# Attention and mixture of experts on one core: banks, probability, scaling and weight splits in another order

## The chip, the core and the metric

The kernel runs on one core of a Trainium2 chip. The metric is the device time of one execution in microseconds (us). Engines go by the profile's names: PE is TensorE (matmuls and transposes), DVE VectorE, ACT ScalarE, POOL GpSimd and SP SyncE; the last two mostly issue transfers here. Before the change the median of three runs is 726.74 us (725.18 to 727.03).

## What is computed

Attention in chunks of 64 tokens over 8 batches, 8 heads and 576 tokens gives 4608 tokens of 512 numbers. A layer of eight experts follows: each token goes through the expert that the gate, or the token before it, names, and the result is scaled with the gate's probability of that expert.

```python
x = attention(q, k, v)                    # (8, 576, 512), in chunks of 64
logits = x @ w_gate                       # 8 experts
e = argmax(logits[b, s]) if s == 0 or sigmoid(x[b, s] @ w_local) < 0.5 else prev_e
p = exp(logits - max); p /= sum(p) + 1e-9
h = maximum(x[b, s] @ w1[e], 0)           # 512 -> 1024
out[b, s] = p[e] * (h @ w2[e])            # 1024 -> 512
```

## The kernel before

The first part of the span (to about 215 us) is the attention, the gate and the sorting of tokens by expert. Then come **units**, numbered u = 0 to 23 here: `step(u)` is called for each in a loop over u, and later calls find nothing to do. A unit holds up to two tiles of 128 tokens of one expert. Its kind is read at run time from a table into registers, and branches select the work:

- a **pair** unit has two full tiles: u = 1, 3, 5 to 8, 10, 13, 14, 17 to 19, 22, 23. `couple` (L788) does the first layer of both tiles in 96 matmuls of 256 columns, in four groups of 24, one PSUM bank each. The results are split into a high and a low part, ACT's `activation` (L806) and DVE's `scalar_tensor_tensor` (L809).
- a **single** unit has one tile (u = 12, 15, 21; u = 0 does this without a branch): 24 matmuls (L656), then transposes in `single` (L768).
- a **partial** unit has up to 64 tokens (u = 11, 16, 20) or 32 (u = 2, 4, 9), the first of an expert. It multiplies the raw weights (L664, L677), while the weights are split for the units behind it.

Every product of a pair or single unit is made of three passes with split operands: weights `w1h`, `w1l` and `w2h`, `w2l` (high and low), tokens `xpp`, hidden values `hab` and `hb`. `split` (L106) makes a quarter of a weight: an ACT cast (L107) of the high part, then a DVE subtraction (L108) of the low one. `refill(0, u)` splits w1 and `refill(1, u)` w2 behind a branch on `turn[u]` (L1038): it is taken where the next unit starts another expert, after u = 1, 3, 8, 10, 14, 15 and 19. If the next unit is partial, `refill(0, u)` makes three quarters, and `partial` in `upper_layer` makes the fourth in the next unit. `reload` fetches raw weights of a later expert.

The order of the work on each engine is the order of the program text (a manual schedule); no planner moves it. For one unit it is: the gate's probability of u (`prob_atoms`, L640 to L647, with one exponential on ACT, L642); the first layer; `x_parts(u+1)`, which transposes the next unit's tokens on PE (L746, one bank of four transposes or two) and splits or copies them (L719, L720, L724, L725); the gather for u+2; `refill(0, u)`; `reload(0, u)`; `lower_layer(u-1)`, the second layer (L670 or L677) of the unit before, its scaling on DVE (L1121, or L703 to L706) and its scatter (L820 on POOL); `hidden(u)`, which for a pair runs `refill(1, u-1)` and then the second layer of the pair's first tile, called **y0** here, scaled at L1151, and for the rest transposes the hidden values and runs `refill(1, u-1)`.

A tile's readers wait by counts of finished instructions on the engine that wrote it. A tile that was written in a branch is ready for its readers when the writer's engine is past that branch, taken or not: these waits show in the trace as DVEq or ACTq L1038.

Of the kernel before, what the change touches and what calls it, by code (L numbers as in the profile page):

```python
# [14 lines left out]
ALU = mybir.AluOpType  # L15
# [3 lines left out]
ET = mybir.EngineType  # L19
# [13 lines left out]
NU = E + (N + (E - 1) * (P - 1)) // (2 * P)  # L33
UMIN = N // (2 * P) - 1
LAST = UMIN + 7
# [36 lines left out]
def tile_attention_then_moe(ctx: ExitStack, tc, q, k_in, v, wg, wl, w1, w2, out):  # L72
# [18 lines left out]
    w1h = [wpool.tile([P, F], F32R, name=f"w1h{c}") for c in range(4)]  # L91
# [14 lines left out]
    def split(hi, lo, raw, lo_eng=None):  # L106
        nc.scalar.copy(hi, raw)  # L107
        (lo_eng or nc.vector).tensor_tensor(lo, raw, hi.bitcast(F32), ALU.subtract)  # L108
# [229 lines left out]
    V = nc.vector  # L338
# [8 lines left out]
    def trp():  # L347
        return ps_tr.tile([P, 512], F32, name="tr")
# [150 lines left out]
    def run(fns):  # L499
        for fn in fns:  # L500
            fn()
# [129 lines left out]
    def prob_atoms(xg, hot):  # L631
        k = xg.shape[1]
        Lg = xg[:, :, C:C + E]
        m = pc.tile([P, 2], F32, name="pm")[:, 0:k]
        ex = pc.tile([P, 2, 2, E], F32, name="pex")[:, :, 0:k]
        sm = pc.tile([P, 2, 2], F32, name="psm")[:, :, 0:k]
        pr = pc.tile([P, 2], F32, name="ppr", bufs=4)
        wide = [P, k, E]
        return pr, [
            lambda: V.tensor_reduce(m, Lg, AX.X, ALU.max),  # L640
            lambda: V.tensor_tensor(ex[:, 0], Lg, m.unsqueeze(2).to_broadcast(wide), ALU.subtract),  # L641
            lambda: nc.scalar.activation(ex[:, 0], ex[:, 0], AF.Exp),  # L642
            lambda: V.tensor_tensor(ex[:, 1], ex[:, 0], hot.unsqueeze(1).to_broadcast(wide), ALU.mult),
            lambda: V.tensor_reduce(sm, ex, AX.X, ALU.add),  # L644
            lambda: V.tensor_scalar(m, sm[:, 0], 1e-9, None, ALU.add),
            lambda: V.reciprocal(m, m),
            lambda: V.tensor_tensor(pr[:, 2 - k:2], sm[:, 1], m, ALU.mult),  # L647
        ]
# [24 lines left out]
    def mm2_part(hf, y, fs):  # L673
        n = C // 2
        for f in fs:
            for j in range(2):
                nc.tensor.matmul(y[HT * j:HT * j + HT, 0:n], hf[:, f % 4, HT * (f // 4):HT * (f // 4) + HT],  # L677
                                 raw2[f // 2][:, f % 2, n * j:n * j + n], start=(f == 0), stop=(f == 7))
# [22 lines left out]
    def y_part(ysb, y, pr):  # L701
        n = C // 2
        V.memset(ysb[HT:P], 0.0)  # L703
        V.tensor_scalar(ysb[0:HT, 0:n], y[0:HT, 0:n], pr[0:HT], None, ALU.mult)
        V.tensor_copy(ysb[0:HT, n:C], y[HT:P, 0:n])
        V.tensor_scalar(ysb[0:HT, n:C], ysb[0:HT, n:C], pr[0:HT], None, ALU.mult)  # L706
# [82 lines left out]
        either(kind[u] and kind[u][1], plain, partial, True)  # L789

    def couple(u, hs):
        banks = [trp(), trp()] + hs
        dsts = h_slot(0), hps[u]
        for g, ps in enumerate(banks):
            for m in range(2):
                f = 2 * g + m
                for c in range(4):
                    for n, (a, w) in enumerate(PASSES):
                        nc.tensor.matmul(  # L799
                            ps[:, 256 * m:256 * m + 256], W1[w][c][:, P * f:P * f + P],  # L800
                            xpp[:, a, c].rearrange("p t q -> p (t q)"),
                            start=(c == 0 and n == 0), stop=(c == 3 and n == 2))
            ps = ps.rearrange("p (f t q) -> p t f q", f=2, t=2)
            parts = [[d[g // 2][a][:, g % 2 * 2:g % 2 * 2 + 2] for a in range(2)] for d in dsts]
            for half in range(2):
                nc.scalar.activation(parts[half][0], ps[:, half], AF.Relu)  # L806
            for half in range(2):
                hi, lo = parts[half]
                V.scalar_tensor_tensor(lo, ps[:, half], 0.0, hi.bitcast(F32), ALU.max, ALU.subtract)  # L809

    def new_ysb(own=False):
        return pc.tile([P, C], F32, name="ysb", **own_tag("ysb", own))
# [235 lines left out]
    def sub(v, engines):  # L1048
        hs = type(v.val)([h for h in v.val.handles if h.engine in engines])
        return type(v).of_register_unchecked(hs, min_val=0, max_val=3)  # L1050
# [17 lines left out]

    def kind_of(u):
        v = flag(3, u, [ET.PE, ET.Activation, ET.DVE, ET.Pool])  # L1070
        return v, sub(v, [ET.PE, ET.Activation, ET.DVE]), sub(v, [ET.Activation, ET.DVE])

    @contextmanager
    def when(v, otherwise=None):
# [11 lines left out]
    def upper_layer(u):  # L1086
        hs, hsb = new_h()
        v = kind[u] and kind[u][1]
        xg = xgs["u", u]
        prc[u], atoms = prob_atoms(xg if v is not None else xg[:, 1:2], ehot[:, u])  # L1090
        run(atoms)

        def plain():
            for c in range(4):
                mm1(x_slot(1), hs, c)
            relu(hsb, hs)

        def partial(M):
            mm1_part(xfs[u], hs, M)
            relu_part(hsb, hs, M)  # L1100
            split(w1h[3], w1l[3], raw1[3])

        if v is None:
            plain()
        else:
            with tc.If(v > 0) as cmp:
                either(v, plain, partial, True)
            with cmp.Else():
                couple(u, hs)
        return hsb  # L1110

    def lower_layer(u):
        y = new_y()
        keep = u + 1 == LAST
        ysb = new_ysb(u + 1 > LAST)
        pr = prc[u][:, 1:2]

        def plain():
            for c in range(4):
                mm2(hps[u], y, c)  # L1120
            V.tensor_scalar(ysb, y, pr, None, ALU.mult)  # L1121

        def partial():
            mm2_part(hfs[u], y, range(8))
            y_part(ysb, y, pr)

        with when(ok[u], (lambda: V.memset(ysb, 0.0)) if keep else None):
            either(kind[u] and kind[u][1], plain, partial)
            if not keep:
                put_y(q_of[u], ysb)  # L1130
        if keep:
            kept.append((q_of[u], ysb))

    def hidden(u, hsb):
        def second():
            if u:
                refill(1, u - 1)

        if kind[u] is None:
            single(u, hsb)  # L1140
            second()
            return
        with tc.If(kind[u][0] > 0) as cmp:
            single(u, hsb)
            second()
        with cmp.Else():
            second()
            y, ysb = new_y(0), new_ysb(u > LAST)
            for c in range(4):
                mm2(h_slot(0), y, c)  # L1150
            V.tensor_scalar(ysb, y, prc[u][:, 0:1], None, ALU.mult)  # L1151
            put_y(q_of[u] - 1, ysb)

    def step(u):
        if u == LAST + 1:
            with when(ok[u]):
                gather_full(u + 1)
        if u < NU:
            hps[u] = h_slot(1, u % 2)
            hfs[u] = pc.tile([P, 4, P], F32, name="hf", **own_tag("hf", u == LAST))  # L1160
            with when(ok[u]):
                hsb = upper_layer(u)
                if u + 1 < NU:
                    xfs[u + 1] = x_parts(u + 1)
        if u != LAST and u + 2 < NU:
            with when(ok[u + 1]):
                gather_full(u + 2)
        if u + 1 < NU:
            refill(0, u)
            reload(0, u)  # L1170
        if u + 2 < NU:
            if u + 2 not in kind:
                kind[u + 2] = kind_of(u + 2)
            turns(u + 1)
        lower_layer(u - 1)
        if u < NU:
            with when(ok[u]):
                hidden(u, hsb)
            if u:
                reload(1, u - 1)  # L1180

# [3 lines left out]
    with tc.manual_schedule(engines=MAN | {ET.SP, ET.Pool}):  # L1185
        kind, ok = {-1: None, 0: None, 1: kind_of(1)}, {u: None for u in range(-1, UMIN)}
        q_of = {u: Q0 + 2 * u + 1 for u in range(NU)} | {-1: EARLY - 1}
        hps[-1], hfs[-1], prc[-1] = h_slot(0), None, prc["e", EARLY - 1]
        turns(0)
        play(PAR["seam"], queues, part_played)  # L1190
        for u in range(LAST + 1):
            step(u)
            n = u + UMIN - 8
            if UMIN <= n < NU:
                ok[n] = valid(n)
                kind[n] = kind_of(n)
            run([sl[0:2], sl[2:3]][u] if u < 2 else [])
        with when(ok[LAST]):
            for u in range(LAST + 1, NU + 1):
                step(u)  # L1200
        for q, ysb in reversed(kept):
            put_y(q, ysb)
# [21 lines left out]
```

## Time and profile before

| | us |
|---|---|
| median of three runs | 726.74 |
| profiled execution, device time | 726.0 |
| its span | 724.1 |
| PE busy in the span | 639.8 (88%) |
| DVE busy | 352.8 (49%) |
| ACT busy | 244.3 (34%) |
| POOL busy | 157.1 (22%) |
| units, 215.0 to 724.1: length | 509.1 |
| units: PE busy | 449.5 |

The profiled execution spent 1.9 us outside its span, and its mean granted PE clock is 0.952 of full speed. PE works through every unit in turn, and the other engines serve it. What counts is therefore how long PE stands still between two pieces of its work, and in which stretches its granted clock is 0.50, where a matmul takes twice as long. The rows of that are in the section behind the next one.

### The profile page before, as it was taken

The numbers are of one execution on the slowest core, as the hardware profiler recorded it, in microseconds if no ns is written. First come the engines' busy times: TensorE is split into PE (matmuls) and PEld (weight loads), VectorE is DVE, ScalarE is ACT, GpSimd is POOL, SyncE is SP. The second block draws the span as 40 slices with busy tenths as digits, with TensorE's granted clock in tenths as the row PEclk, the third lists the DMA queues.
The fourth block names the chain that finished last, engine by engine and source line by source line (L and its number), as shares of the span: only waits on it lengthen the run. The fifth ranks groups of instructions, "written<-read, shape, count | busy, mean of one in ns | idle before, by whom it ended". The sixth has DMA issues, their size and how long they took to land. (4 is left out here: it accounts for less than half of the span.)

```text
span 724.1 us, 16913 instructions
## 1 busy us (share of the span) xinstructions
PE 639.8 (88%) x6136; PEld 530.1 (73%) x6136; DVE 352.8 (49%) x909; ACT 244.3 (34%) x461; POOL 157.1 (22%) x226
## 2 busy tenths in 40 slices
PE   6789999889899797799999797899987999979993
PEld 5668788666689585588889594698756798668882
DVE  3656778866966444253223354642464432353220
ACT  4557777563123132141113132420343221242110
POOL 4313232740231211112111211212021112121101
PEclk9989999999999988899999899999997999999997
DMA  8999999997141143614011242751336231055000
GB/s 225 244 228 241 243 248 271 265 315 236 59 161 47 42 151 92 218 49 164 31 47 45 61 158 69 249 170 60 134 95 238 76 125 60 31 174 174 31 19 34
DMA packets 103571, 100.98 MB, mean 139 GB/s; under 512 B 42488, under 2 KB 79352, under 8 KB 103416
## 3 DMA queue, kind: packets, MB, share of 16 engines
q1 hardware_dynamic: 88584, 61.01, 30.3%
q0 software_dynamic: 7440, 23.32, 9.9%
q10 hardware_dynamic: 7392, 14.68, 6.3%
q8 instruction: 85, 1.39, 0.8%
q14 instruction: 70, 0.57, 0.3%
HBM read 79.95 MB, written 20.35 MB: 139 GB/s over the span
## 5 line engine op out<-in xcount | busy, mean ns | idle before, releaser
L670 PE MATMUL y<-w2h,hab 128*128 128x512 f32 x432 | 149.1, 418 | 5.7 <-ACTq L1038 3.9
L820 POOL DMA_INDIRECT out<-ysb,sidx x41 | 41.0, 1001 | 363.3 <-DVEq L1038 160.2
L670 PEld LDWEIGHTS y<-w2h,hab 128*128 128x128 f32 x432 | 86.6, 201 | 29.1 <-ACTq L1038 5.6
L670 PE MATMUL y<-w2l,hab 128*128 128x512 f32 x216 | 91.4, 423 | 17.8 <-DVEq L1038 17.8
L799 PE MATMUL tr<-xpp,w1h 128*128 128x256 f32 x448 | 84.8, 287 | 3.1 <-DVE hf L173 1.9
L799 PE MATMUL h<-xpp,w1h 128*128 128x256 f32 x448 | 82.9, 283 | 0.0
L642 ACT ACTIVATE pex<-pex 128x16 f32<-128x16 f32 (+1 forms) x27 | 5.9, 217 | 205.1 <-DVE pex L641 184.4
L799 PEld LDWEIGHTS tr<-xpp,w1h 128*128 128x128 f32 x448 | 71.9, 194 | 3.8 <-ACT hf L171 2.1
L799 PEld LDWEIGHTS h<-xpp,w1h 128*128 128x128 f32 x448 | 70.8, 192 | 0.0
L670 PEld LDWEIGHTS y<-w2l,hab 128*128 128x128 f32 x216 | 43.3, 201 | 32.6 <-DVEq L1038 23.1
L799 PE MATMUL tr<-xpp,w1l 128*128 128x256 f32 x224 | 64.2, 286 | 0.0
L626 POOL DMA_INDIRECT xg<-x_d,gidx x49 | 48.4, 988 | 70.0 <-DVE psm L644 31.6
L799 PE MATMUL h<-xpp,w1l 128*128 128x256 f32 x224 | 63.4, 283 | 0.0
L1151 DVE TENSOR_SCALAR ysb<-y,ppr 128x512 f32<-128x512 f32 x14 | 10.5, 751 | 86.8 <-PE y L670 86.8
L1121 DVE TENSOR_SCALAR ysb<-y,ppr 128x512 f32<-128x512 f32 x19 | 14.3, 750 | 70.0 <-PE y L670 55.9
L746 PE MATMUL tr<-ident,xg 128*128 128x128 f32 x156 | 24.8, 295 | 21.6 <-issue 18.4
L799 PEld LDWEIGHTS tr<-xpp,w1l 128*128 128x128 f32 x224 | 43.5, 194 | 0.4
L670 PE MATMUL y<-w2h,hb 128*128 128x512 f32 x128 | 43.6, 412 | 0.0
L799 PEld LDWEIGHTS h<-xpp,w1l 128*128 128x128 f32 x224 | 42.9, 192 | 0.0
L809 DVE SCALAR_TENSOR_TENSOR hab<-h,hab 128x256 fp32r<-128x256 f32 x44 | 17.1, 420 | 50.7 <-ACT hab L806 27.9
L108 DVE TENSOR_TENSOR w1l<-raw,w1h 128x1024 fp32r<-128x1024 f32 x28 | 33.0, 1221 | 12.7 <-ACT w1h L107 12.6
L746 PEld LDWEIGHTS tr<-ident,xg 128*128 128x128 f32 x156 | 18.9, 150 | 27.6 <-issue 22.4
(259 smaller groups left out, 1142.3 us busy)
## 6 DMA issues: line engine op xcount, KB each, us to landing
raw<-in_moe_w SPq DMA_DIRECT2D x14, 1024.0 KB
raw<-in_moe_w ACTq DMA_DIRECT2D x14, 1024.0 KB
raw<-in_moe_w SPq DMA_DIRECT2D x16, 512.0 KB
qt<-in_q SPq DMA_DIRECT2D x11, 512.0 KB
kt<-in_k SPq DMA_DIRECT2D x11, 512.0 KB
v<-in_v SPq DMA_DIRECT2D x22, 256.0 KB
x_d<-xs SPq DMA_DIRECT2D x7, 521.0 KB
x_d<-x_w2h SPq DMA_DIRECT2D x6, 521.0 KB
```

The costliest lines, as they stand in the source:

```text
L108: (lo_eng or nc.vector).tensor_tensor(lo, raw, hi.bitcast(F32), ALU.subtract)
L626: nc.gpsimd.indirect_dma_start(out=dst, out_offset=None, in_=src, in_offset=bass.IndirectOffsetOnAxis(ap=gidx[t].bitcast(U32), axis=0))
L642: lambda: nc.scalar.activation(ex[:, 0], ex[:, 0], AF.Exp),
L670: nc.tensor.matmul(y, hx[f // 4][a][:, f % 4], W2[w][c][:, f % 2, :], start=(f == 0 and n == 0), stop=(f == 7 and n == 2))
L746: nc.tensor.transpose(ps[:, n], xg[:, half, P * n:P * n + P], ident)
L799: nc.tensor.matmul(ps[:, 256 * m:256 * m + 256], W1[w][c][:, P * f:P * f + P], xpp[:, a, c].rearrange("p t q -> p (t q)"), start=(c == 0 a ...
L809: V.scalar_tensor_tensor(lo, ps[:, half], 0.0, hi.bitcast(F32), ALU.max, ALU.subtract)
L820: nc.gpsimd.indirect_dma_start(out=out, out_offset=bass.IndirectOffsetOnAxis(ap=sidx[t].bitcast(U32), axis=0), in_=ysb, in_offset=None, bo ...
L1121: V.tensor_scalar(ysb, y, pr, None, ALU.mult)
L1151: V.tensor_scalar(ysb, y, prc[u][:, 0:1], None, ALU.mult)
```

## The change

Six things stand elsewhere in the program. (1) `couple` fills the two `h` banks first and the two `tr` banks last. (2) The probability of u moves from the start of the unit to `side_work(u)`, behind `x_parts(u+1)`. (3) So does the fourth quarter of the w1 split, in a branch of its own (L1136), and `refill(0, u)` of units that are not pairs. (4) For pairs `refill(0, u)` moves into the pair's branch of `hidden(u)`, behind `refill(1, u-1)`. (5) The scaling and the scatter of u-1 become `lower_out` and stand behind `hidden(u)`. (6) `reload(0, u)` comes at the end of the step. Two further registers hold the kind for PE alone and for DVE alone, as the branches of `lower_layer` and `lower_out` are now taken apart. No matmul, cast, subtraction, scaling or transfer is added or removed. Of branch instructions executed there are more: on DVE 257 compares for 219 and 254 jumps for 209, on ACT 258 and 254 for 243 and 209, on PE 171 and 245 for 164 and 209.

```diff
     def couple(u, hs):
-        banks = [trp(), trp()] + hs
+        banks = hs + [trp(), trp()]
...
     def upper_layer(u):
         hs, hsb = new_h()
         v = kind[u] and kind[u][1]
-        xg = xgs["u", u]
-        prc[u], atoms = prob_atoms(xg if v is not None else xg[:, 1:2], ehot[:, u])
-        run(atoms)
...
         def partial(M):
             mm1_part(xfs[u], hs, M)
             relu_part(hsb, hs, M)
-            split(w1h[3], w1l[3], raw1[3])
...
+    def side_work(u):
+        xg = xgs["u", u]
+        prc[u], atoms = prob_atoms(xg if kind[u] else xg[:, 1:2], ehot[:, u])
+        run(atoms)
+        if kind[u]:
+            with tc.If(kind[u][2] > 0):
+                with tc.If(kind[u][2] > 1):
+                    split(w1h[3], w1l[3], raw1[3])
+                renew(0, u)
+        else:
+            renew(0, u)
...
         with tc.If(kind[u][0] > 0) as cmp:
             single(u, hsb)
-            second()
+            renew(1, u - 1)
         with cmp.Else():
-            second()
+            renew(1, u - 1)
+            renew(0, u)
             y, ysb = new_y(0), new_ysb(u > LAST)
...
                     xfs[u + 1] = x_parts(u + 1)
+                side_work(u)
...
-        if u + 1 < NU:
-            refill(0, u)
-            reload(0, u)
...
-        lower_layer(u - 1)
+        run(more)
+        y = lower_layer(u - 1)
         if u < NU:
             with when(ok[u]):
                 hidden(u, hsb)
+        lower_out(u - 1, y)
+        if u < NU:
+            if u + 1 < NU:
+                reload(0, u)
             if u:
                 reload(1, u - 1)
```

In the rows below a name stands for an instruction's output and inputs: `ysb` a scaled tile, `y` its PSUM bank, `raw` raw weights, `tr` and `h` banks of PSUM.

First DVE at the end of `hidden(3)`, in the program before: the branch of `refill(1, 2)` in the pair's half, then y0's scaling.

```order
L1038 COMPARE_AND_BRANCH
L108 TENSOR_TENSOR w2l<-raw_0_85,w2h 128x1024 x2
L108 TENSOR_TENSOR w2l<-raw_1_86,w2h 128x1024 x2
L1038 UNCONDITIONAL_BRANCH x2
L1151 TENSOR_SCALAR ysb<-y,ppr 128x512
L1143 UNCONDITIONAL_BRANCH
L1059 UNCONDITIONAL_BRANCH
```

The same place in the program after, from behind `refill(1, 2)`; the scaling of unit 2 (L703 to L706 or L1124) follows these rows.

```order
L1038 COMPARE_AND_BRANCH
L108 TENSOR_TENSOR w1l_77<-raw_0_83,w1h_73 128x1024
L108 TENSOR_TENSOR w1l_78<-raw_0_83,w1h_74 128x1024
L108 TENSOR_TENSOR w1l_79<-raw_1_84,w1h_75 128x1024
L1078 COMPARE_AND_BRANCH
L108 TENSOR_TENSOR w1l_80<-raw_1_84,w1h_76 128x1024
L1078 UNCONDITIONAL_BRANCH x2
L1038 UNCONDITIONAL_BRANCH
L1159 TENSOR_SCALAR ysb<-y,ppr 128x512
L1150 UNCONDITIONAL_BRANCH
L1059 UNCONDITIONAL_BRANCH
```

A w1 split now stands in the pair's half of `hidden`, and the other half has none. The last writer of `w1h` and `w1l` therefore stands in one half of that branch.

Next DVE ahead of `hidden(3)` in the program before: the scaling of unit 2, either way.

```order
L690 COMPARE_AND_BRANCH
L703 MEMSET ysb 64x512
L704 TENSOR_SCALAR ysb<-y,ppr 64x256
L705 COPY ysb<-y 64x256
L706 TENSOR_SCALAR ysb<-ysb,ppr 64x256
L690 UNCONDITIONAL_BRANCH
L1121 TENSOR_SCALAR ysb<-y,ppr 128x512
L690 UNCONDITIONAL_BRANCH
L1143 COMPARE_AND_BRANCH
```

And in the program after, between `x_parts(4)` and `hidden(3)`.

```order
L640 TENSOR_REDUCE pm<-xg 128x2
L690 UNCONDITIONAL_BRANCH
L641 TENSOR_TENSOR pex<-xg,pm 128x16
L643 TENSOR_TENSOR pex<-pex,ehot 128x16
L644 TENSOR_REDUCE psm<-pex 128x4
L645 TENSOR_SCALAR pm<-psm 128x2
L646 RECIPROCAL pm<-pm 128x2
L647 TENSOR_TENSOR ppr<-psm,pm 128x2
L1135 COMPARE_AND_BRANCH
L1136 COMPARE_AND_BRANCH
L108 TENSOR_TENSOR w1l_80<-raw_1_84,w1h_76 128x1024
L1136 UNCONDITIONAL_BRANCH x2
```

The scaling is gone from there, and the probability and the fourth quarter of w1 have come.

Last DVE in the first layer of unit 3, before: the low parts of `couple`, by bank.

```order
L1106 COMPARE_AND_BRANCH
L690 COMPARE_AND_BRANCH
L692 COMPARE_AND_BRANCH
L108 TENSOR_TENSOR w1l_80<-raw_1_84,w1h_76 128x1024
L692 UNCONDITIONAL_BRANCH
L108 TENSOR_TENSOR w1l_80<-raw_1_84,w1h_76 128x1024
L692 UNCONDITIONAL_BRANCH
L690 UNCONDITIONAL_BRANCH
L809 SCALAR_TENSOR_TENSOR hab<-tr,hab 128x256 x4
L809 SCALAR_TENSOR_TENSOR hab<-h_4759,hab 128x256 x2
L809 SCALAR_TENSOR_TENSOR hab<-h_4760,hab 128x256 x2
```

And after.

```order
L1102 COMPARE_AND_BRANCH
L690 COMPARE_AND_BRANCH
L692 COMPARE_AND_BRANCH
L692 UNCONDITIONAL_BRANCH x2
L690 UNCONDITIONAL_BRANCH
L809 SCALAR_TENSOR_TENSOR hab<-h_4780,hab 128x256 x2
L809 SCALAR_TENSOR_TENSOR hab<-h_4781,hab 128x256 x2
L809 SCALAR_TENSOR_TENSOR hab<-tr,hab 128x256 x4
L1102 UNCONDITIONAL_BRANCH
L751 COMPARE_AND_BRANCH
```

The `tr` banks, which `x_parts` uses next, are now read out last.

## Rows read from the trace of the kernel before

**Rows 1.** The page, its first part: busy time, share, instructions.

```profile
PE 639.8 (88%) x6136; PEld 530.1 (73%) x6136; DVE 352.8 (49%) x909; ACT 244.3 (34%) x461; POOL 157.1 (22%) x226
```

**Rows 2.** Waits of PE, 215 to 724: in total, times, longest, in us.

```profile
PE tr L746 <- issue: 18.4, 5, 7.0
PE y L670 <- DVEq L1038: 17.8, 14, 3.1
PE y L670 <- ACTq L1038: 3.9, 2, 2.0
PE tr L746 <- ACT w1h L107: 2.8, 1, 2.8
PE tr L799 <- DVE hf L173: 1.9, 1, 1.9
PE tr L799 <- DVE hf L725: 1.2, 1, 1.2
```

**Rows 3.** By stretch: length, PE busy, PEclk, DMA share, GB/s; granted clock 0.50.

```profile
296.02:302.85 6.83, 4.73 (x13) 0.50 0.61 215
309.67:313.09 3.42, 3.42 (x18) 0.50 0.08 28
...
541.78:552.02 10.24, 5.34 (x15) 0.50 0.81 277
...
sum 47.79, PE 37.92; mean PE 4.74
```

**Rows 4.** Timeline, DVE and PE, around y0: start, length, instruction, [idle before].

```profile
283.05 0.79 PE L670 MATMUL y<-w2l,hab 128*128 128x512 f32 x1 [3.08 <-DVEq L1038]
...
351.82 0.75 DVE L1121 TENSOR_SCALAR ysb<-y,ppr 128x512 f32<-128x512 f32 x1 [3.85 <-PE y L670]
352.68 0.51 PE L670 MATMUL y<-w2l,hab 128*128 128x512 f32 x1 [0.73 <-DVEq L1038]
```

**Rows 5.** Timeline, DVE and PE, the second bank of x_parts in partial units.

```profile
250.69 0.16 DVE L647 TENSOR_TENSOR ppr<-psm,pm 128x2 f32<-128x2 f32 x1
251.28 1.22 DVE L108 TENSOR_TENSOR w1l<-raw,w1h 128x1024 fp32r<-128x1024 f32 x1 [0.43 <-ACT w1h L107]
252.60 1.09 PE L746 MATMUL tr<-ident,xg 128*128 128x128 f32 x4 [3.15 <-issue]
...
537.23 4.63 DVE L108 TENSOR_TENSOR w2l<-raw,w2h 128x1024 fp32r<-128x1024 f32 x4
546.68 1.09 PE L746 MATMUL tr<-ident,xg 128*128 128x128 f32 x4 [6.96 <-issue]
```

**Rows 6.** Timeline, unit 6: x_parts(7) behind couple, the last low part, the split of x.

```profile
345.06 1.04 PE L746 MATMUL tr<-ident,xg 128*128 128x128 f32 x8
346.36 0.41 DVE L809 SCALAR_TENSOR_TENSOR hb<-h,hb 128x256 fp32r<-128x256 f32 x1
346.69 1.28 DVE L720 TENSOR_TENSOR xpp<-tr,xpp 128x512 fp32r<-128x512 f32 x2
```

**Rows 7.** Timeline, from hidden(4) into couple(5).

```profile
298.12 1.09 PE L746 MATMUL tr<-ident,xg 128*128 128x128 f32 x4 [4.21 <-issue]
306.38 0.38 PE L768 MATMUL tr<-ident,hsb 128*128 128x128 f32 x2
307.99 3.89 ACT L107 CAST w2h<-raw 128x1024 fp32r<-128x1024 f32 x4
308.67 0.36 PE L799 MATMUL tr<-xpp,w1h 128*128 128x256 f32 x1 [1.90 <-DVE hf L173]
309.07 4.63 DVE L108 TENSOR_TENSOR w2l<-raw,w2h 128x1024 fp32r<-128x1024 f32 x4 [0.86 <-ACT w2h L107]
```

**Rows 8.** By stretch, all engines: plain pair unit 6; busy in the order PE, PEld, DVE, ACT, POOL.

```profile
333.50:358.20 24.70, 23.97 (x154) 21.38 (x153) 6.82 (x19) 3.82 (x11) 3.95 (x4) 1.00 0.26 87
```

**Rows 9.** Timeline of PE, x_parts in unit 12; then that stretch as rows 8.

```profile
468.34 0.63 PE L746 MATMUL tr<-ident,xg 128*128 128x128 f32 x4 [1.78 <-issue]
...
464.00:475.00 11.00, 8.91 (x68) 6.88 (x68) 7.34 (x18) 4.12 (x8) 2.47 (x3) 1.00 0.32 97
```

More of the change, by code (lines that the diff above doesn't have):

```diff
@@ L1070, in kind_of @@
         v = flag(3, u, [ET.PE, ET.Activation, ET.DVE, ET.Pool])
-        return v, sub(v, [ET.PE, ET.Activation, ET.DVE]), sub(v, [ET.Activation, ET.DVE])
+        return v, sub(v, [ET.PE, ET.Activation, ET.DVE]), sub(v, [ET.Activation, ET.DVE]), sub(v, [ET.PE]), sub(v, [ET.DVE])
     @contextmanager
@@ L1113, in lower_layer, with plain, lower_out @@
         y = new_y()
+        def plain():
+            for c in range(4):
+                mm2(hps[u], y, c)
+        with when(ok[u]):
+            either(kind[u] and kind[u][3], plain, lambda: mm2_part(hfs[u], y, range(8)))
+        return y
+    def lower_out(u, y):
         keep = u + 1 == LAST
@@ L1116, in lower_layer @@
         pr = prc[u][:, 1:2]
[L1118 to L1125, printed above, removed]
         with when(ok[u], (lambda: V.memset(ysb, 0.0)) if keep else None):
-            either(kind[u] and kind[u][1], plain, partial)
+            either(kind[u] and kind[u][4], lambda: V.tensor_scalar(ysb, y, pr, None, ALU.mult), lambda: y_part(ysb, y, pr))
             if not keep:
@@ L1132, in lower_layer, with renew @@
             kept.append((q_of[u], ysb))
+    def side_work(u):
[9 more added lines that the diff above has]
+            renew(0, u)
+    def renew(which, u):
+        if 0 <= u < NU - 1:
+            refill(which, u)
     def hidden(u, hsb):
-        def second():
-            if u:
-                refill(1, u - 1)
         if kind[u] is None:
             single(u, hsb)
-            second()
             return
@@ L1144, in hidden @@
             single(u, hsb)
-            second()
+            renew(1, u - 1)
         with cmp.Else():
-            second()
+            renew(1, u - 1)
+            renew(0, u)
             y, ysb = new_y(0), new_ysb(u > LAST)
@@ L1152, in hidden, with step @@
             put_y(q_of[u] - 1, ysb)
-    def step(u):
+    def step(u, more=()):
         if u == LAST + 1:
@@ L1191, in tile_attention_then_moe @@
         for u in range(LAST + 1):
-            step(u)
+            step(u, [sl[0:2], sl[2:3]][u] if u < 2 else ())
             n = u + UMIN - 8
@@ L1196, in tile_attention_then_moe @@
                 kind[n] = kind_of(n)
-            run([sl[0:2], sl[2:3]][u] if u < 2 else [])
         with when(ok[LAST]):
```

## The prediction

> **What bounds the kernel now.** I read the page's first part first: PE is busy for 639.8 of 724.1 us, the next engine, DVE, for 352.8 [rows 1]. PE goes through all units in turn, so the time is PE's work, plus its pauses, plus what half clock adds. The change adds and removes no arithmetic, so only the last two can move. Second come the waits of PE from 215 us on [rows 2]. Two families carry them. Transposes of `x_parts` (`tr` L746) wait 18.4 us in five places, with no releaser shown, and 2.8 in a sixth. The second layer (`y` L670) waits 17.8 us in 14 places for DVE and 3.9 in two for ACT to pass the branch at L1038. Two waits of `couple` for the copy of `hf` make 3.1. Third come the stretches at a granted clock of 0.50, that is 1.2 of 2.4 GHz: eight of them, 47.79 us with PE busy for 37.92 [rows 3]. Half of that busy time, 19.0 us, is what they cost. Before each, PE had stood still for 1.9 us or more: 4.21 us before 298.12, for instance, and 1.90 before 308.67 [rows 7]. In plain pair units, with pauses of about 0.7 us, the clock stays at 1.00 [rows 4, 8], and it does not fall behind the pause of 1.78 before 468.34 [rows 9].
>
> The sum starts from the profiled execution, 726.0 us, within 0.1% of the median of 726.74.
>
> **The y0 waits (parts 2, 4, 5).** In a plain pair unit DVE scales the tile of u-1 when its second layer is done (351.82, 0.75 long), and only then passes the branch of `refill(1, u-1)`, for which the low weights of y0 wait: PE starts them at 352.68 [rows 4]. After, the scaling stands behind y0. Ahead of the branch DVE now has the low parts, `x_parts` and the probability. From the end of `couple` these take 1.7 us to the end of the last L809, then 1.28 for the two L720 [rows 6] and about 1.6 for seven small instructions of 0.16 or little more (as at 250.69 [rows 5]) with one exponential on ACT among them: some 5 to 7 us with branches and with the wait of part 1. PE needs 6.8 for `x_parts` and the second layer of u-1 (345.06 to 351.82 [rows 4, 6]) and the pause of part 1 before it comes to the low weights, so the wait goes. Behind a partial unit the second layer of u-1 has 32 short matmuls (L677) for 24 long ones and is some 2 us shorter; there, at u = 3, 5, 10 and 17, I leave about 1 us each. The worst of the old waits are among these: at 283.05 the four instructions L703 to L706 of a partial tile's scaling stood ahead of the branch, 3.08 us [rows 4]. So 17.8 + 3.9 - 4.0 = 17.7 us go. Starting PE again after each pause costs some 0.2 beside the pause, and one more wait of L677 goes: 3 more. Bounds: 12 (all units keep 0.6) to 24.
>
> **The second bank of x_parts in partial units (parts 3, 5).** Before, it needs the engine past the branch of the partial first layer, and the last thing in that branch is the fourth quarter of the w1 split, behind the probability: 251.28 + 1.22, and PE starts at 252.60 [rows 5]. After, the split stands behind `x_parts`, and DVE reaches that point after the scalings of the unit before, each 0.75. At u = 2, 4 and 9 I leave 0.7 each. At u = 16 DVE is behind with four w2 subtractions (4.63 us from 537.23 before, and PE waits 6.96) [rows 5]; in the new order three w1 subtractions stand ahead of these, and I leave 5. At u = 12 and 21 the pause moves to the weights (below), and I leave 0.5 each. Of 18.4 + 2.8 = 21.2 some 8.1 stay, so 13.1 go. Bounds: 8 to 18.
>
> **The banks of couple (part 1).** The first bank of `couple` no longer is the one that the copies of `hf` read: 3.1 us go [rows 2]. The price is at its end. In unit 6 the transposes of `x_parts(7)`, two banks, follow `couple` at 345.06 without a pause, while the last low part ends at 346.36 + 0.41 = 346.77 [rows 6]. That low part reads an `h` bank before and the second `tr` bank after. The second bank's four transposes, now at about 345.42, can then start at 346.85: 1.4 us. It holds for each pair unit whose successor has two banks: u = 5, 6, 7, 13, 17, 18, 22 and 23, so 8 x 1.4 = 11.5 us. With one bank in the successor nothing waits. Bounds: 8 (nothing but the last bank's tail, 1.0 each) to 14.
>
> **Where w1 is last written (part 4).** The last writer of `w1h` and `w1l` now stands in the pair's half of `hidden`. PE's wait is a count of ACT and DVE instructions, and where the other half ran, the built program reaches that count with what stands there: read in its waits, `couple` of u = 3, 5, 10 and 17 has its four high quarters released by the four w2 casts of the partial unit's `hidden`, and its low ones by the `hf` copy and the first three w2 subtractions. Before, the same matmuls wait for a branch that is long past. In `hidden(4)` PE's transposes end at 306.76; the casts run from 307.99, four in 3.89, and the subtractions from 309.07, four in 4.63 [rows 7], so the third ends at about 312.5. DVE's scaling ahead of them goes, but ACT and DVE copy `hf` in turns, so I move nothing. All quarters are needed by the first 12 matmuls, which took 1.4 us; the eleventh would start at 307.95 and starts at 312.5: 4.55 us, in four units 18.2. Bounds: nothing (the count is met early) to 22. Such a pause takes the clock with it: of 6.83 us at half speed after the 4.21 us pause, 4.73 were work [rows 3, 7], which costs 2.4; in parts with a little work between I take 1.8, so 7.2. Bounds: 0 to 12. The single units 12 and 21, which use the quarters more slowly, lose 1.4 each, and the pairs 13 and 22 behind them wait for a low part of `hb`, about 1.4 each: 5.6. Bounds: 0 to 7.
>
> **Clock, end, branches.** With the old pauses gone, only the stretch at 541.78 stays of the eight (half of 5.34 is 2.7) [rows 3]: 19.0 - 2.7 = 16.3 us go, 12 at the least. At the end the last second layer waits for y0's scaling; another, 0.75 [rows 4], now comes after that one and is waited for too: 0.9 more. No row prices the branches that PE executes more, 43 in 509 us; I take 2 us, between 0 and 4, and nothing for those of DVE and ACT, which are idle for more than half of a unit [rows 8]. The queues: on POOL the gather for u+2 fills the buffer that the probability of u reads, so it starts some 3 us later, and the scatter of u-1 comes behind that of y0; POOL is busy for 3.95 of 24.70 us of a unit [rows 8], and a gather has a whole unit until it is used: nothing, and up to 1 us in a unit if a transfer is slow. On SP `reload(0, u)` comes at the end of the step; it is needed two units later: nothing.
>
> **Sum.** 17.7 + 3 + 13.1 + 3.1 + 16.3 = 53.2 go; 11.5 + 18.2 + 7.2 + 5.6 + 0.9 + 2 = 45.4 come. 726.0 - 7.8 = 718, and 718.6 on the median's scale. Two large numbers nearly cancel, so the sign is less sure than either.
>
> **Rivals.**
> *The waits on w2 are not there* (faster). If the count is reached early, 18.2 + 7.2 fall out: 718 - 25 = 693 us. For it: such a wait shows nowhere in the trace before. Against it: the built program. Chance 0.15.
>
> *The short pauses bring the clock down* (slower). Each of the eight new pauses of 1.4 us stands between a full `couple` and a full second layer. If each is followed by a stretch like that at 309.67, 3.42 us of work at half speed [rows 3], it costs 1.7 more: 8 x 1.7 = 13.7, and 732 us. From five of the eight on the kernel is slower than before or level with it. Against it: the pause of 1.78 that left the clock alone [rows 9] and plain pair units at 1.00 [rows 8]. For it: 1.90 was enough once. Chance 0.17.
>
> The Trainium skill, TensorE: Matmul & The Clock Gate, section "A second HAM failure mode: psum-queue depth-cycling", says that PE, cycling through PSUM banks, can pause shortly but so often that the clock swings between its levels. This speaks against part 1, which adds a pause at a bank in eight units, and by it the time would be this rival's. The trace so far bears it out at 1.90 us and not at 0.7 to 1.8.
>
> *DVE is late* (no change). If DVE reaches the branch at `x_parts` later than I take it, since y0 and the tile before are scaled just ahead of it, 3 to 4 us of wait stay at u = 2, 4 and 9, with half clock in two of them: 9 or so, and 726 us. For it: L1151 and the scaling are 1.5 us in a row, with branches between. Chance 0.13.
>
> **How the numbers follow.** The forecast, 718, has 0.45, and 0.1 is left for what I don't see, on either side. Its own range, from the bounds of its terms, is 708 to 726. With part of the first two rivals, the range that leaves out 2 in 10 is 702 to 733. A measurement can tell about 0.3%, 2.2 us. Within that of 726.7 lie most of the third rival and a little of the forecast: 0.13. Slower by more: the second rival and some of the rest, 0.2. Faster by more: 0.67.
>
> **What would show it.** In the profile after: `y` L670 for DVEq L1038 falls from 14 waits to a few of 1 us; `tr` L746 waits eight times for DVE `hab` or `hb` L809, 1.4 us each; `h` L799 waits for ACT `w2h` and DVE `w2l` in four units, 4 to 5 us together in each; half clock stands behind those and near u = 16 only. The prediction is wrong if the L799 waits on w2 are missing, if PEclk falls behind the waits for L809, or if partial units keep pauses above 3 us ahead of `x_parts`' second bank.

## The result: slower by 0.7%

The changed kernel takes 732.32 us in the median of 20 runs (728.07 to 737.96), the kernel before 728.0 in 20 runs beside them (724.25 to 732.03). The ratio is 1.0069, with a 95% interval of 1.0045 to 1.0093. The two profiled executions differ by more, 731.2 to 724.1 us of span, 7.1 us; part of that is the spread of single executions. One thing more than the six stands elsewhere: the sorting of later tokens, `run(more)` in the diff (L587 on PE), comes ahead of the second layer in units 0 and 1, and came behind these units before.

The waits of PE in the changed kernel, from 215 us on, are the counterpart of [rows 2]:

```profile
PE tr L746 <- issue: 15.6, 10, 3.8
PE h L799 <- ACT w2h L107: 9.3, 7, 2.3
PE h L799 <- ACTq L1038: 3.9, 2, 2.1
PE h L656 <- issue: 3.3, 2, 1.7
PE y L670 <- DVE xpp L720: 2.1, 1, 2.1
PE y L670 <- ACT xpp L719: 2.1, 2, 1.5
PE y L670 <- DVEq L1038: 1.7, 4, 0.6
PE y L670 <- DVEq L1078: 1.6, 1, 1.6
PE tr L587 <- DVE pm L640: 1.4, 1, 1.4
```

The 14 y0 waits of 17.8 us have become four of 1.7. In their place stand waits of `couple` for the w2 split (9.3) and for a branch on ACT (3.9), and the transposes of `x_parts` wait in ten places for five, the longest 3.8 us for 7.0.

What a pause costs is more than its idle row: in unit 6 below, a row of 1.20 us makes `x_parts` 1.88 us longer, and behind some pauses the granted clock falls to half. So I took each piece of PE's work in units 1 to 23 (a `couple`, an `x_parts`, a second layer) from its start to the start of the next, and took away what the same piece takes undisturbed in these traces: 11.52 us for a `couple`, 5.66 for 24 second-layer matmuls, 0.79 or 0.35 for `x_parts` with two banks or one. What is left over, in us, and the time from the start of the last second layer to the end of the span:

| | x_parts | second layers | couple, L656, L768 | L664 | sum | last y to end |
|---|---|---|---|---|---|---|
| before | 25.7 | 41.3 | 6.5 | 2.9 | 76.3 | 16.5 |
| changed | 29.3 | 10.7 | 38.4 | 2.2 | 80.6 | 19.6 |

30.6 us went from the second layers, and 31.9 came to `couple` and what leads to it. 3.6 came to `x_parts` and 3.1 to the end. With 0.7 less at L664 and 0.3 less ahead of unit 1 that makes 7.0, the difference of the spans but for rounding.

**Couple behind a partial unit.** The timeline of unit 4's `hidden` and `couple` of unit 5 in the changed kernel, ACT, DVE and PE (start, length, instruction, idle before), beside [rows 7]:

```profile
296.55 0.38 PE L768 MATMUL tr<-ident,hsb 128*128 128x128 f32 x2
298.10 3.89 ACT L107 CAST w2h<-raw 128x1024 fp32r<-128x1024 f32 x4
299.18 4.63 DVE L108 TENSOR_TENSOR w2l<-raw,w2h 128x1024 fp32r<-128x1024 f32 x4 [0.86 <-ACT w2h L107]
299.20 0.39 PE L799 MATMUL h<-xpp,w1h 128*128 128x256 f32 x1 [2.27 <-ACT w2h L107]
300.15 0.39 PE L799 MATMUL h<-xpp,w1h 128*128 128x256 f32 x1 [0.33 <-ACT w2h L107]
...
302.73 0.58 PE L799 MATMUL h<-xpp,w1l 128*128 128x256 f32 x1
```

The first matmul starts when the first cast of w2 is done (298.10 + 1.05), the fourth (300.15) with the second. The low parts go by the subtractions: the eleventh matmul starts at 302.73, when the third subtraction is done, and without a wait it would have started at about 297.9. What they read is w1, whose last quarter DVE finished at 294.64. From 301.75 to 305.17 the granted clock is 0.50, and a matmul's row there is 0.41 long where it is 0.28 at full clock.

**The second bank of x_parts behind couple.** Unit 6 in the changed kernel, PE and DVE, beside [rows 6]:

```profile
338.26 0.60 PE L746 MATMUL tr<-ident,xg 128*128 128x128 f32 x4
339.55 0.41 DVE L809 SCALAR_TENSOR_TENSOR hb<-tr,hb 128x256 fp32r<-128x256 f32 x1
340.06 0.63 PE L746 MATMUL tr<-ident,xg 128*128 128x128 f32 x4 [1.20 <-issue]
340.93 0.47 PE L670 MATMUL y<-w2h,hab 128*128 128x512 f32 x1 [0.24 <-issue]
```

The second four transposes wait for the last low part, which ends at 339.96. `x_parts` takes 2.67 us for 0.79: 1.4 of waiting, and then some. The trace's records of PE's sequencer, which issues PE's instructions and runs its branches, show what follows the wait: the sequencer stands until 340.0, and only then loads a register and passes the compare (the instruction that decides a branch) ahead of the second layer, from 340.56 to 340.76. Where PE does not wait, the same instructions are passed while PE still works: in experiment 1 this compare ends at 341.32, before `x_parts` starts at 341.76, and costs PE nothing.

**The end.** The last scatters on POOL, before and then changed:

```profile
701.38 0.97 POOL L820 DMA_INDIRECT out<-ysb,sidx  x1 [17.03 <-DVEq L1038]
707.94 0.97 POOL L820 DMA_INDIRECT out<-ysb,sidx  x1 [5.59 <-DVEq L1078]
714.64 0.97 POOL L820 DMA_INDIRECT out<-ysb,sidx  x1 [5.73 <-DVEq L1078]
```

```profile
711.04 0.97 POOL L820 DMA_INDIRECT out<-ysb,sidx  x1 [22.66 <-DVE ysb L1159]
714.65 0.97 POOL L820 DMA_INDIRECT out<-ysb,sidx  x1 [2.64 <-DMA out<-ysb,sidx]
721.35 0.97 POOL L820 DMA_INDIRECT out<-ysb,sidx  x1 [5.73 <-DVEq L1078]
```

The scatter of u-1 now comes right behind that of y0 and waits until that transfer has landed, starting 3.6 us behind it; the last comes 6.70 us later, as before. DVE had scaled the last tile by 718.41, so the last scatter waits for POOL's queue and not for DVE.

### The profile page after: what moved, and what is told of

Same layout as the page of the kernel before. It is cut to its first block, busy times and chain, and to the rows that moved or that the text cites. A ratio compares the mean times of both kernels' runs of the same rounds, so it can differ in the third digit from the quotient of the medians.

```text
span 731.2 us, 17067 instructions
## 1 busy us (share of the span) xinstructions
PE 647.6 (89%) x6136; PEld 536.8 (73%) x6136; DVE 352.3 (48%) x909; ACT 246.4 (34%) x461; POOL 159.0 (22%) x226
## 5 line engine op out<-in xcount | busy, mean ns | idle before, releaser
L670 PE MATMUL y<-w2h,hab 128*128 128x512 f32 x432 | 144.3, 407 | 5.6 <-DVE xpp L720 2.1
L799 PE MATMUL h<-xpp,w1h 128*128 128x256 f32 x448 | 96.5, 310 | 13.5 <-ACT w2h L107 9.3
L820 POOL DMA_INDIRECT out<-ysb,sidx x41 | 41.3, 1007 | 271.3 <-DVE ysb L1159 126.1
L799 PEld LDWEIGHTS h<-xpp,w1h 128*128 128x128 f32 x448 | 80.6, 215 | 16.9 <-ACT w2h L107 11.9
L670 PE MATMUL y<-w2l,hab 128*128 128x512 f32 x216 | 87.5, 405 | 1.7 <-DVEq L1038 1.7
L799 PE MATMUL h<-xpp,w1l 128*128 128x256 f32 x224 | 70.5, 315 | 1.3 <-DVEq L1038 0.8
L806 ACT ACTIVATE hab<-h 128x256 fp32r<-128x256 f32 x44 | 15.1, 382 | 150.4 <-PE h L799 137.6
L1159 DVE TENSOR_SCALAR ysb<-y,ppr 128x512 f32<-128x512 f32 x14 | 10.5, 751 | 85.1 <-PE y L670 85.1
L799 PEld LDWEIGHTS h<-xpp,w1l 128*128 128x128 f32 x224 | 47.9, 214 | 4.3 <-DVE w2l L108 2.5
L809 DVE SCALAR_TENSOR_TENSOR hab<-tr,hab 128x256 fp32r<-128x256 f32 x44 | 17.2, 421 | 59.5 <-ACT hab L806 34.0
L656 PE MATMUL h<-w1h,xpp 128*128 128x512 f32 x112 | 34.9, 413 | 3.3 <-issue 3.3
```

What stands on the lines that cost most here:

```text
L656: nc.tensor.matmul(hs[j], xs[a][:, c], W1[w][c][:, 512 * j:512 * j + 512], start=(c == 0 and n == 0), stop=(c == 3 and n == 2))
L670: nc.tensor.matmul(y, hx[f // 4][a][:, f % 4], W2[w][c][:, f % 2, :], start=(f == 0 and n == 0), stop=(f == 7 and n == 2))
L799: nc.tensor.matmul(ps[:, 256 * m:256 * m + 256], W1[w][c][:, P * f:P * f + P], xpp[:, a, c].rearrange("p t q -> p (t q)"), start=(c == 0 a ...
L820: nc.gpsimd.indirect_dma_start(out=out, out_offset=bass.IndirectOffsetOnAxis(ap=sidx[t].bitcast(U32), axis=0), in_=ysb, in_offset=None, bo ...
```

## The experiments

The theory after the result: the change takes away the y0 waits as forecast, and gives them back in three places of its own, `couple` behind a partial unit (the place where w1 is last written), the second bank of `x_parts` (the bank order) and the end (the scatter's place). The rival: the added branches slow all engines, and pauses only change their names. Each kernel was run 4 to 10 times beside the kernel before on the same chip, so ratios are compared; the kernel before had medians of 722 to 730 us there. The changed kernel was timed for the result alone, so what stands below against it is a difference of two ratios.

**1. The banks alone, in the changed kernel.**

```diff
-        banks = hs + [trp(), trp()]
+        banks = [hs[0], trp(), trp(), hs[1]]
```

> The changed kernel with its banks in the order h, tr, tr, h, so that both tr banks are read out before couple ends; nothing else. Theory (the eight pauses ahead of the second bank of x_parts, 1.8 to 2.2 us each in the changed kernel's trace, are part of what is lost): these eight go, and the half clock behind two of them, about 16 + 3 us, so 732 becomes 711 to 717, and no wait for hf comes back. Rival (what is lost is spread over the added branches, and another wait takes the place of these): 727 to 733.

Measured: 717.31 us, ratio 0.9899 (0.9851 to 0.9948), so 1.7% or 12 us below the changed kernel's ratio. `x_parts` falls from 29.3 to 12.9 in the accounting above; the rest nearly stays (second layers 11.2, `couple` 36.4). The eight pauses are gone: in unit 6 both banks are one row again, and the second layer follows.

```profile
341.76 1.04 PE L746 MATMUL tr<-ident,xg 128*128 128x128 f32 x8
342.55 0.48 PE L670 MATMUL y<-w2h,hab 128*128 128x512 f32 x1
```

Little took their place: 0.6 us each at a second layer in units 5 and 17. A pause of 1.4 us ahead of L587 at u = 1 went with them. The theory's sign and place hold. By the ratio the size, 12, is below the 15 to 21 expected; in the profiled executions the pauses fell by 17.4.

**2. The banks alone, in the kernel before.** With the change's order:

```diff
-        banks = [trp(), trp()] + hs
+        banks = hs + [trp(), trp()]
```

> The kernel before with the bank order of the change alone, h first. Theory: the waits for hf go (-3), eight pauses ahead of the second bank of x_parts come, 1.4 to 2 each with half clock behind a few, so 8 to 16 us above the kernel before. Rival (the pauses cost only in the new order of the rest, before they are covered by the y0 wait that follows): within 3 us of the kernel before.

Measured: 738.37 us, ratio 1.0207 (1.0150 to 1.0265), 15 us slower, inside the range. The transposes of `x_parts` wait in 14 places for five (PE's waits):

```profile
PE tr L746 <- issue: 28.4, 14, 7.0
PE y L670 <- DVEq L1038: 17.8, 14, 3.1
```

The pause at the bank is as long as in the changed kernel, and the y0 waits behind it are the 17.8 us of [rows 2] still: this part alone costs some 2% of the kernel. With the order h, tr, tr, h on the kernel before:

> The kernel before with the banks in the order h, tr, tr, h. Theory: the two waits for hf go, 3 us, and the half clock behind one, 1.7; no pause comes: 2 to 5 us below the kernel before. Rival (the copies of hf are waited for at the second bank, too): level with it.

Measured: 723.65 us, ratio 1.0009 (0.9964 to 1.0054), level with it. Of the theory's 2 to 5 us, 5 is outside the interval and 2 inside. The trace settles the waits: in two places, u = 5 and 17, `couple` still waits, now for ACT's w2 casts by name (4.1 us), so the 3.1 us of part 1 were not to be had by the order. What they were stands in the section on the prediction.

**3. One place for the w1 split.**

```diff
-            with tc.If(kind[u][2] > 0):
-                with tc.If(kind[u][2] > 1):
-                    split(w1h[3], w1l[3], raw1[3])
-                renew(0, u)
-        else:
-            renew(0, u)
+            with tc.If(kind[u][2] > 1):
+                split(w1h[3], w1l[3], raw1[3])
+        renew(0, u)
...
             renew(1, u - 1)
-            renew(0, u)
             y, ysb = new_y(0), new_ysb(u > LAST)
```

> The changed kernel with the w1 split of a turning unit in one place for every kind, behind the probability in side_work, and none in the pair's half of hidden. Theory (couple behind a partial unit waits for the w2 split because w1 has its last writer in one half of a branch): the four couples of u = 3, 5, 10, 17 fall from 15 to 16 us to about 11.6, with the wait ahead of them, 25 us together, and 8 us go at u = 12, 13, 21, 22. Back come waits of y0 for the branch in the six pairs that turn, 2 to 4 us each with half clock behind most, 17 to 27 us. In all 722 to 731. Rival (couple waits for its tokens or for hf): the couples stay at 15 us and the time at 732 or above.

Measured: 732.95 us, ratio 1.0115 (1.0043 to 1.0187), level with the changed kernel and above the 722 to 731 expected. The couples are as the theory says: `couple`, L656 and L768 fall from 38.4 to 5.4, all four couples take less than 11.7 us. The y0 waits in the turning pairs come back in full, second layers 10.7 to 38.8:

```profile
PE y L670 <- ACTq L1038: 10.8, 5, 3.5
PE y L670 <- DVEq L1038: 7.7, 8, 1.5
```

So part 4 is an exchange of one wait for another of nearly the same size. The run settles that the place of w1's last write makes `couple` wait, but gains nothing. At u = 12 PE also waited 4.0 us for a gather, with half clock behind it, which is no part of the theory. The next run takes away the couples' wait without bringing the y0 waits back.

**4. The w2 split behind the branch.**

```diff
         with tc.If(kind[u][0] > 0) as cmp:
             single(u, hsb)
-            renew(1, u - 1)
         with cmp.Else():
             renew(1, u - 1)
             renew(0, u)
...
+        with tc.If(kind[u][2] > 0):
+            renew(1, u - 1)
```

> The changed kernel with one difference: where a unit is not a pair, its w2 split stands behind the branch of hidden, not in its first half, so the count that the next couple waits for on w1 is reached at the end of that half, ahead of the split. Theory (couple waits for the w2 split through the count): couple of u = 3, 5, 10, 17 goes from 15 to 16 us to 11.6 to 13, the wait ahead of it goes, 18 to 25 us together, and 6 to 8 at u = 12, 13, 21 and 22; no y0 wait comes back, against the kernel with one place for w1. In all 25 to 33 us below the changed kernel: 695 to 707. Rival (those couples wait for something else that ends as late, the hf copies or the tokens): within 5 us of the changed kernel.

Measured: 717.98 us, ratio 0.982 (0.977 to 0.9869), 2.5% or 18 us below the changed kernel. `couple`, L656 and L768 fall from 38.4 to 14.7, 23.7 us, and no wait on w2 is left in the list of PE's waits; the second layers stay at 13.6. With experiment 3 that shows the count as the cause: here w1 stays where the change put it, the split of w2 has the same length, and only stands behind the branch for what stood in one half of it. At u = 5 a pause is left, 4.1 of 6.0 us with its half clock:

```profile
297.92 0.36 PE L799 MATMUL h<-xpp,w1h 128*128 128x256 f32 x1 [2.28 <-issue]
```

The time fell by less than the 25 to 33 us expected, as this stayed and `x_parts` and second layers took 6 us more, most of it at u = 9, 12 and 21.

**5. Both.** Experiments 1 and 4 in one kernel.

> The changed kernel with the first two mends, banks h, tr, tr, h and the w2 split behind the branch; scaling and scatter stay behind y0. Theory (the gains of the two add, as they are pauses in different places): 14 us by the one and 13 by the other in the spans, so about 27 to 31 below the changed kernel, and the end, from the last second layer on, keeps its 19.6 us, 3 longer than in the kernel with three mends. Rival (they hide each other): no more than 20 below it.

Measured: 698.93 us, ratio 0.9578 (0.9549 to 0.9607): 4.9% or 36 us below the changed kernel, for 27 to 31 expected, and 4.2% below the kernel before. The sum of the pauses is 46.8 us for 80.6, 34 less, where experiments 1 and 4 alone had 17 and 16 less. The gains add; the pauses had not hidden each other. The branches that the change adds are all still there, so the rival, by which they are what is lost, is out. The end keeps its length (19.2 us), with the wait of the scatter still in it:

```profile
681.29 0.97 POOL L820 DMA_INDIRECT out<-ysb,sidx  x1 [18.99 <-DVEq L1160]
685.33 0.97 POOL L820 DMA_INDIRECT out<-ysb,sidx  x1 [3.06 <-DMA out<-ysb,sidx]
692.03 0.97 POOL L820 DMA_INDIRECT out<-ysb,sidx  x1 [5.73 <-issue]
```

**6. And the end.** Experiments 1 and 4, with the w2 split and y0 moved behind the scaling and scatter of u-1. Against the changed kernel, besides the banks:

```diff
         with tc.If(kind[u][0] > 0) as cmp:
             single(u, hsb)
-            renew(1, u - 1)
         with cmp.Else():
             renew(1, u - 1)
             renew(0, u)
+
+    def last_part(u):
+        if kind[u] is None:
+            return
+        with tc.If(kind[u][0] > 0) as cmp:
+            renew(1, u - 1)
+        with cmp.Else():
             y, ysb = new_y(0), new_ysb(u > LAST)
...
         lower_out(u - 1, y)
         if u < NU:
+            with when(ok[u]):
+                last_part(u)
```

> The changed kernel with three places mended at once: banks h, tr, tr, h; the w2 split of units that are not pairs behind the branch; the scaling and scatter of u-1 ahead of y0 and behind the branches on new weights. Theory: the gains of the first two add, 17 and 25 to 33 us, and the end (the last second layer to the end of the span) falls from 19.6 to 16.5 us, as the scatter of u-1 no longer stands behind that of y0. About 50 below the changed kernel: 676 to 690. Rival (the pauses hide each other and others take their place): no more than 30 us below it, 700 or above.

Measured: 702.59 us, ratio 0.9647 (0.9571 to 0.9723), 31 us below the changed kernel: the rival's time, not the 50 of the theory. Its interval overlaps that of experiment 5, so this third mend shows no gain in time. The end does fall to 16.7 us, as the theory says; the scatters now stand 6 to 7 us apart:

```profile
677.91 0.97 POOL L820 DMA_INDIRECT out<-ysb,sidx  x1 [17.82 <-DVE ysb L1124]
684.29 0.97 POOL L820 DMA_INDIRECT out<-ysb,sidx  x1 [5.40 <-DVEq L1078]
691.07 0.97 POOL L820 DMA_INDIRECT out<-ysb,sidx  x1 [5.81 <-DVEq L1078]
```

But y0 stands in a second branch now, and PE waits at it in every plain pair, some 0.75 us at u = 6, 7 and 13 and 1.5 at 18, 22 and 23, before it can load y0's first weights:

```profile
339.04 0.47 PE L670 MATMUL y<-w2h,hab 128*128 128x512 f32 x1 [0.56 <-PEq L1150]
```

**7. The scaling alone, in the kernel before** (part 5; `lower_out` as in the change, behind `hidden(u)`, with the two further registers).

> The kernel before with part 5 alone: scaling and scatter of u-1 behind hidden(u). Theory: the y0 waits of plain pair units (0.95 us each in six units) go, those at u = 3 and 10 lose the 2 us of the partial tile's scaling and some half clock, about 2 go at the other turning pairs; at the end the scatter costs 3.2 more and the wait for y0's scaling 0.8. In all 5 to 14 us below the kernel before. Rival (the branch alone, or the instructions behind it, hold y0, not the scaling): level with the kernel before or 3 us above it.

Measured: 720.01 us, ratio 0.9888 (0.9834 to 0.9942), 8 us faster, inside the range. The y0 waits for DVE fall from 14 to 6:

```profile
PE y L670 <- DVEq L1038: 5.6, 6, 1.4
```

Second layers fall from 41.3 to 25.2, and the end grows from 16.5 to 20.6 us. This is the gain of the change, with its price at the end.

**8. The fourth quarter alone, in the kernel before** (part 3).

```diff
             relu_part(hsb, hs, M)
-            split(w1h[3], w1l[3], raw1[3])
...
                     xfs[u + 1] = x_parts(u + 1)
+                if kind[u]:
+                    with tc.If(kind[u][2] > 1):
+                        split(w1h[3], w1l[3], raw1[3])
```

> The kernel before with part 3 alone: the fourth quarter of the w1 split behind x_parts, in a branch of its own; the probability and the scalings stay where they were. Theory (the second bank of x_parts in partial units waits for the branch with that split): the pauses ahead of it, 3.15 us at u = 2, 4.21 at u = 4, 2.85 at u = 9, 2.3 at u = 21, fall to 1 or less, and the half clock behind them goes; at u = 16 some 2 us stay less. In all 10 to 18 us below the kernel before. Rival (DVE and ACT are late with the probability and the scalings, the split is only last in the row): 0 to 6 us below.

Measured: 719.88 us, ratio 0.9871 (0.9822 to 0.9921), 9 us faster, just short of the 10 to 18 expected. At u = 4 the pause goes as forecast, 4.21 to 0.61 us; at u = 2 `x_parts` still takes 2.6 us too long, at u = 9 2.6 us are left, at u = 16 5.56 of the 6.96 us wait, and at u = 21, where I had counted on 2, nothing changed.

## Why the prediction was wrong

The forecast was 7.8 us faster; the profiled executions say 7.0 slower, and the 20 runs 4.3. The steps, in their order:

- **The y0 waits: right.** 1.7 us are left, in the four pairs that were named, for 4.0 forecast. Experiment 7 shows the scaling as what held y0 in most places.
- **The wait of couple on w2: right, to the number.** Wait and half clock together were 6.6, 6.0, 6.4 and 6.4 us at u = 3, 5, 10 and 17: 25.4, for 18.2 + 7.2. The eleventh matmul came 4.8 us late at u = 5, for the 4.55 of the prediction.
- **The two waits for hf: misread.** I took 3.1 us of the kernel before for waits on the copies of `hf`. In the records of PE's sequencer a compare stands ahead of each of these couples (L1106): it ends at 308.50 at u = 5, after 5.43 us, and at 556.79 at u = 17, after 3.48, and `couple` begins 0.17 us behind each. So it does in experiment 2 with either order of the banks, and in experiment 7. In experiment 8, with the old order, `couple` of u = 5 begins while the copies still run:

```profile
302.36 0.36 PE L799 MATMUL tr<-xpp,w1h 128*128 128x256 f32 x1 [0.69 <-DVE ysb L1120]
...
302.83 0.29 DVE L173 COPY hf<-tr 128x128 f32<-128x128 f32 x1 [0.33 <-ACT hf L171]
```

  So PE stood at a branch there, whatever the order. In the changed kernel the wait on w2 covers it; the pause that experiment 4 leaves at u = 5 is this one, behind a compare of 5.72 us.
- **The second bank in partial units: mis-sized.** I left 8.1; the rows at u = 2, 4, 9, 16 and 21 keep 9.3, and 11.3 with what follows them. Another 3.4 came at u = 1 and 11, where I had seen nothing. At u = 1 it is the banks again: `run(more)` has brought L587 right behind `x_parts`, and it starts only when the last low part of `couple` is out of the `tr` bank, at 233.44. With the `tr` banks in the middle this pause is gone (experiments 1, 5 and 6), with them last it stays (3 and 4). At u = 11 the wait is put down to `xpp`, but PE's sequencer shows a branch instead: the compare ahead of the second layer lasts 3.74 us, 1.85 in the kernel before. So it is at u = 9: the compare behind the first layer (L692) lasts 3.03 us, and 3.73 in the kernel before, where I had read the 2.85 as a wait for the split; experiment 8 moved the split and left it. The 2.1 us at u = 2 have no such compare, and stay open. My 2 us for branches, which no row had priced, lie in these places.
- **The eight pauses at the banks: price too low.** The wait is the 1.4 us that I worked out, but the second layer behind it starts late, too, by 0.2 to 0.6, the time of PE's compares behind the wait: one at u = 6, five at u = 18 and 22. `x_parts` costs 1.8 to 2.2 us more in place of 1.4: 16.0 for 11.5.
- **The rival of the clock came in part.** At u = 22 and 23 half clock follows the pause at the bank, 1.5 us each, and at the other six not. That is one of the signs that the prediction named against itself; another, a pause above 3 us in a partial unit, came at u = 16 alone (3.8), where I had left 5.
- **Pairs behind single units: three times too low.** The 1.4 us that I gave u = 13 and 22 were 4.3 and 4.4. `couple` waits not for a low part only, but for ACT to pass the branch at L1038, and half clock follows. With w1 in one place (experiment 3) neither couple waits, so this, too, comes of the place of w1's last write. With u = 12 and 21: 12.5 for 5.6.

```profile
467.10 0.38 PE L799 MATMUL h<-xpp,w1h 128*128 128x256 f32 x1 [1.84 <-ACTq L1038]
467.78 0.39 PE L799 MATMUL h<-xpp,w1l 128*128 128x256 f32 x1 [0.30 <-DVEq L1038]
```

- **The queues: "nothing" was wrong.** I looked at POOL's busy share, and missed that the scatter of u-1 would wait for that of y0 to land. In the middle of the kernel no wait of PE names it; at the end it is 3.1 us on the span. Experiments 6 and 7 show it from both sides. The gathers were put at nothing, too: that holds in the changed kernel, but in experiments 3 and 5 PE waited 4.0 and 3.5 us for one at u = 12.

The clock stretches in the changed kernel, at the first, the two behind single units and the two at u = 22 and 23 (length, PE busy, PEclk, DMA share, GB/s), beside [rows 3]:

```profile
260.50:267.40 6.90, 6.46 (x27) 0.52 0.70 248
...
469.00:472.40 3.40, 3.40 (x18) 0.50 0.74 225
...
653.50:656.90 3.40, 2.94 (x15) 0.52 0.34 74
670.50:673.90 3.40, 3.40 (x9) 0.51 0.15 44
697.90:701.30 3.40, 3.40 (x10) 0.53 0.01 2
sum 44.40, PE 41.92; mean PE 4.66
```

Nine stretches of 44.40 us stand for eight of 47.79; half of PE's busy time in them is 21.0 us, for 19.0 before. I had one old stretch stay and four come, 9.9 us.

The sum by place, in us: what the accounting gives, and what the prediction's terms make of it when the 16.3 us of clock go where PE's work at half clock lay (2.2 in `x_parts`, 12.4 in second layers, 1.7 in `couple`).

| | before | forecast | changed |
|---|---|---|---|
| x_parts and L664 | 28.6 | 24.8 | 31.5 |
| second layers | 41.3 | 9.1 | 10.7 |
| couple, L656, L768 | 6.5 | 32.7 | 38.4 |
| last second layer to the end | 16.5 | 16.5 | 19.6 |
| branches, at no place | | 2.0 | |
| sum | 92.9 | 85.1 | 100.2 |

So `x_parts` is off by 6.7, of which the banks are 4.5; `couple` and what leads to it by 5.7, of which the units behind and ahead of single units are 6.9, with 1.2 less elsewhere; the end by 3.1; the second layers by 1.6. Less the 2 for branches, which lie in these places, and 0.3 ahead of unit 1, that is the 14.8 us from 7.8 faster to 7.0 slower. (Two slips in the prediction change nothing: its 11.5 is 8 times 1.43, and 726.74 less 7.8 is 718.9, not 718.6.)

The step that failed is the price of the new waits in the sum: a bank's pause was taken at the length of the wait alone (11.5 for 16.0), the pairs behind single units at a low part's wait (5.6 for 12.5), and the scatter behind y0's at nothing (3.1). Most of the places were right, and the wait on w2 was right in size. But the forecast was a small difference of two sums near 50, and these three, 4.5, 6.9 and 3.1 too low, turned its sign. The rival on the clock had the right sign for two of its eight places only. The mends of the banks and of the count show that these two hold back what the moved scaling and the fourth quarter gain; the mend of the scatter's place shortens the end, but shows no gain in time.

## What to carry to other kernels

When work moves into one half of a branch, look up which count its readers wait for on the other half: a reader can wait for work that has nothing to do with it, and moving that work behind the branch gave 2.5% here. PSUM banks that the next step reuses should not be filled last: in the middle they cost no more than first, and last they cost 1.7 to 2.1%. A wait of PE is to be priced with the branch instructions that stand right behind it and with the clock, not with its idle row: here 1.4 us cost 1.8 to 3.8. And where PE pauses behind a branch, look at its sequencer's own records before the engine that the profile names.

## What the hardware showed beside

Half clock followed two pauses that were shorter than any in the kernel before which it had followed: 1.20 us at the bank and 0.5 to 0.6 behind it, in units 22 and 23. The same two pauses at u = 18 left the clock alone, as did 1.20 and 0.2 at u = 6. Here are u = 18 and then u = 22:

```profile
591.37 0.63 PE L746 MATMUL tr<-ident,xg 128*128 128x128 f32 x4 [1.19 <-issue]
592.50 0.47 PE L670 MATMUL y<-w2h,hab 128*128 128x512 f32 x1 [0.50 <-PE tr L746]
...
668.48 0.63 PE L746 MATMUL tr<-ident,xg 128*128 128x128 f32 x4 [1.20 <-issue]
669.72 0.47 PE L670 MATMUL y<-w2h,hab 128*128 128x512 f32 x1 [0.62 <-ACT xpp L719]
```

So no length of one pause tells here whether the clock falls. The other kernels with the `tr` banks last say the same: half clock followed the pause at the bank at u = 18 in experiment 3, at 17 and 22 in experiment 4, and at none of the eight in experiment 2.

The second is what a compare on PE's sequencer can take. Most take 0.05 to 0.4 us; the ones at u = 5, 9, 11 and 17 that PE waited behind took 3.0 to 5.7. What such a compare waits for its record does not say.

The Trainium skill, Runtime: NRT & Kernel Launch, section "Instruction fetch mechanics", says that a taken branch to code that has not been fetched stalls the engine until it has. These compares agree with it, but no run here changes the place or size of the code alone, so that this was the cause is not shown.
